# Pooled attention and expert routing on one core: values pooled inside their own pair, another order of loads and mixing steps, no unused matmuls

## The chip, the cores and the metric

The kernel runs on one NeuronCore of a Trainium2 chip. The metric is the device time of one execution in microseconds (us); runs are compared by their median. A core has five engines that work side by side, each with a queue that it takes in order: PE (TensorE, matrix products), DVE (VectorE), ACT (ScalarE), POOL (GpSimd, which here issues most DMA transfers) and SP (SyncE, which here issues the writes of one intermediate). PE's weight loads are listed by themselves as PEld.

## What is computed

Batch 8, 8 heads, 576 positions, head size 64. Keys and values are averaged over groups of 8 positions (576 become 72), attention runs against these 72, and its output, 4608 tokens of 512, goes through one of 8 experts of two layers, chosen for each token by a given index.

```python
k_p = k.reshape(B, H, Sp, pool, D).mean(axis=3)      # pool = 8, Sp = 72
v_p = v.reshape(B, H, Sp, pool, D).mean(axis=3)
scores = scale * np.matmul(q, k_p.transpose(0, 1, 3, 2))
attn = np.exp(scores - np.max(scores, axis=-1, keepdims=True))
attn = attn / (np.sum(attn, axis=-1, keepdims=True) + 1e-09)
x = np.matmul(attn, v_p)                             # then (B*S, H*D)
...
for e in range(E):
    mask = domain_id == e
    h = np.maximum(x[mask] @ w1[e], 0.0)
    out[mask] = h @ w2[e]
```

## The kernel before

**Staging.** The attention works on pairs of batches, four pairs (`NP`). For each pair the three inputs are loaded as one tile of 128 partitions each, 1152 KB in half precision (`load_pair`, L78), issued on GpSimd's queue; each of k, q and v has two buffers, so that the load for pair 2 waits until pair 0's tile has been read. All of PE's work is cut into small units, and a plan puts them in order:

- `kp_units` (L373): pools k by 16 matmuls against an identity matrix (L392) and turns the result (L400); two copies out of PSUM for each, on VectorE, or on ScalarE in pair 0 (L383, L385). Six units.
- `vp_units` (L406): nine units pool and turn v by four matmuls each (L421), with three copies on ScalarE (L424); two more units fold pairs of positions into one (L434), with a copy each on ScalarE (L436). The result `vp` has two buffers, the intermediate `vT` one.
- `qt_units` (L440): five units transpose q (L449); four copies on VectorE (L453), one on ScalarE (L451).
- `sc_unit` (L456): scores of one head for all 576 positions, two matmuls (L463), then the exponential on ScalarE (L466). 16 for each pair.
- `av_unit` (L469), here called a mixing step: 8 or 16 matmuls (L483) mix the pooled values by the scores for 128 tokens into the PSUM tile `wide`, of which there is one; VectorE divides by the sums (L487, L489) into `x_sb`. 9 for each pair. After each third one SyncE writes 384 KB to the DRAM buffer `x_lin` (L498).
- `turn_units` (L549): transposes gathered tokens (L557) through a PSUM tile that shares the one buffer of `wide`; VectorE copies it to `xT` (L558).
- `l1_units` (L567) and `l2_units` (L588): the two layers of an expert (L578, L594). The result of the second is scattered to the output by GpSimd (L603).

**Order.** Each unit is put into a list with a number as its time (16 to a pair: pair `pr` has `16*pr` to `16*pr + 16`), the list is sorted, and the units are emitted in that order (L621 to L684). Each engine then takes its instructions in the order of emission. Score units of pair `pr` stand at `16*pr + h`. Mixing steps follow from 8.6 on, 16/9 apart, so that the last five of a pair fall into the next pair's numbers. Pooling and transposing for pair `pr + 1` stand inside pair `pr`: keys, values, queries, in this order (L637 to L641). Pair 0's values are pooled inside pair 0 too (L652).

**Routing.** While the attention runs, VectorE builds from the expert index the row of `x_lin` that each slot of an expert holds: `perm_units` and `perm_mm` for each pair, then `perm_finish` (L355, nine small operations), `orig_finish` (L367, nine) and `count` (L239, with one matmul, L248). Rows are fetched by indirect DMAs (`gather`, L542), five blocks of 128 for each expert. The first three blocks of experts 0 and 1 hold rows of the first three pairs alone, so these six gathers and expert 0's first layer on 384 tokens (`e0_unit`, L677) start while the fourth pair is still mixed.

**GpSimd's queue** is in order as well. Its loads before: k0, q0, v0, k1, v1, q1, then k2, v2, q2, k3, v3, q3, two weight loads (expert 0), six gathers, two weight loads (expert 1), and then gathers, loads and scatters of the expert stage.

**Unused matmuls.** `dummy` (L501) multiplies the identity by a part of k into a PSUM tile that nobody reads. Twelve of them stand at 48.4 to 59.4, in the fourth pair.

Of the kernel before, what the change touches and what calls it, by code (L numbers as in the profile page):

```python
# [20 lines left out]
NP = 4  # L21
NC_ = 9
# [11 lines left out]
XE = 128 * NC_ * EPAIR  # L34
# [5 lines left out]
def kernel(  # L40
# [10 lines left out]
    nc = tc.nc  # L51
# [19 lines left out]
    def small():  # L71
        return ps.tile([128, 512], F32, tag="small", bufs=2, name="small")
# [5 lines left out]
    def load_pair(t_ap, pr, tag):  # L78
        t = wp.tile([128, 72, D], F16, tag=tag, bufs=2, name=tag)
        nc.gpsimd.dma_start(  # L80
            t[:].rearrange("p t d -> p (t d)"),
            t_ap[2 * pr:2 * pr + 2].rearrange("b h (g t) d -> (b h g) (t d)", g=8))
        return t

    with tc.manual_schedule():
# [7 lines left out]
        kt, vt, qt_ = {}, {}, {}  # L93
# [13 lines left out]
        nc.gpsimd.iota(row_i[:], pattern=[[128, NCH]], base=0, channel_multiplier=1)  # L107
        vt[0] = load_pair(v, 0, "v")
        kt[1] = load_pair(k, 1, "k")
        vt[1] = load_pair(v, 1, "v")  # L110
        qt_[1] = load_pair(q, 1, "q")

        iota_f = rt.tile([128, 128], F32, name="iota_f")
        nc.vector.tensor_copy(iota_f[:], iota_row[:])
# [4 lines left out]
        ident = const.tile([128, 128], F16, name="ident")  # L119
# [26 lines left out]
        for cc in range(NC_):  # L146
            if cc <= 4:
                nc.tensor.matmul(Rv[:, :, cc, :], selA[:, 128 * cc:128 * cc + 128], domT[:, :, 0, :],
                                 start=True, stop=(cc < 4), skip_group_check=True)
            if cc >= 4:  # L150
                c0 = 128 * (cc - 4)
                nc.tensor.matmul(Rv[:, :, cc, :], selB[:, c0:c0 + 128], domT[:, :, 1, :],
                                 start=(cc > 4), stop=True, skip_group_check=True)
# [302 lines left out]
        def sc_unit(pr, bh):  # L456
            s = st[pr]
            if bh % 8 == 0:
                s["at", bh // 8] = wk.tile([128, H, S], F16, tag="at", bufs=3, name="at")
            at = s["at", bh // 8]  # L460
            p = big()
            for par in range(2):
                nc.tensor.matmul(p[0:72, par, 0:288], s["kpT"][64 * par:64 * par + 64, bh, :],  # L463
                                 s["qT"][64 * par:64 * par + 64, :, 8 * bh:8 * bh + 8],
                                 start=True, stop=True)
            nc.scalar.activation(at[0:72, bh % 8, :].rearrange("p (a c) -> p a c", a=2),  # L466
                                 p[0:72, :, 0:288], AFT.Exp, scale=1.0 / 64.0)

        def av_unit(pr, cc):  # L469
            s = st[pr]  # L470
            if cc % 3 == 0:
                s["x"] = per.tile([128, 3, HD], F16, tag="x_sb", bufs=4, name="x_sb")
            x_sb = s["x"][:, cc % 3, :]
            pv = wide()
            lo, hi = 128 * cc, 128 * cc + 128
            parts = []
            if lo < S:
                parts.append((0, lo, min(hi, S), 0))
            if hi > S:
                parts.append((1, max(lo, S) - S, hi - S, max(lo, S) - lo))  # L480
            for bt, a, z, r0 in parts:
                for h in range(H):
                    nc.tensor.matmul(pv[r0:r0 + z - a, h, 0:65], s["at", bt][0:72, h, a:z],  # L483
                                     s["vp"][0:72, 8 * bt + h, :], start=True, stop=True,
                                     skip_group_check=True)
            rcp = wk.tile([128, 8], F32, tag="rcp", bufs=4, name="rcp")
            nc.vector.reciprocal(rcp[:], pv[:, :, 64])  # L487

            nc.vector.tensor_tensor(out=x_sb.rearrange("p (b h a) -> p b h a", b=4, h=H),  # L489
                                    in0=pv[:, :, 0:64].rearrange("p h (a b) -> p b h a", b=4),  # L490
                                    in1=rcp[:].unsqueeze(1).unsqueeze(3).to_broadcast([128, 4, 8, 16]),
                                    op=ALU.mult)
            if cc % 3 == 2:
                if pr < EPAIR:
                    rows, c = x_lin[0:XE, :].rearrange("(p c) d -> p c d", c=EC), NC_ * pr + cc - 2
                else:
                    rows, c = x_lin[XE:XROWS, :].rearrange("(p c) d -> p c d", c=LC), NC_ * (pr - EPAIR) + cc - 2
                i = nc.sync.dma_start(rows[:, c:c + 3, :], s["x"][:])  # L498
                tc.declare_no_dep(i.ins, group="xg", reason="the rows gathered so far are of other pairs")

        def dummy():  # L501
            p = small()
            nc.tensor.matmul(p[:], ident[:], kt[NP - 1][:].rearrange("p t d -> p (t d)")[:, 0:512],
                             start=True, stop=True)

        def merge(a, b, start=0.0):

            out_, n = [], len(a)
# [15 lines left out]
        def wload_units(e, which, parts):  # L524
            box = {}

            def unit(i):
                if i == 0:
                    tag = W_AT[e][which]
                    bufs = 4 if tag == "w" else 2  # L530
                    t = wp.tile([128, 4096] if tag == "w" else [128, 72, D], F16, tag=tag, bufs=bufs, name=tag)
                    box["t"] = t[:] if tag == "w" else t[:].rearrange("p t d -> p (t d)")[:, 0:4096]
                    k = (4, 8)[which]
                    box["s"] = (moe_w1, moe_w2)[which][e].rearrange("(p k) f -> p (k f)", k=k)
                    wt.setdefault(e, []).append(box["t"].rearrange("p (k f) -> p k f", k=k))
                c = slice(4096 // parts * i, 4096 // parts * (i + 1))
                nc.gpsimd.dma_start(box["t"][:, c], box["s"][:, c])
            return [lambda i=i: unit(i) for i in range(parts)]
# [3 lines left out]
        def gather(e, j, rows=XROWS):  # L542
            i = nc.gpsimd.indirect_dma_start(  # L543
                out=xg[e % 2][:, j, :], out_offset=None, in_=x_lin[0:rows, :],
                in_offset=bass.IndirectOffsetOnAxis(ap=xrow[:, NBL * e + j:NBL * e + j + 1], axis=0),
                bounds_check=rows - 1, oob_is_err=False)
            tc.add_to_no_dep_group("xg", i.ins)
# [62 lines left out]
        def run(units):  # L610
            for f in units:
                f()
# [9 lines left out]
        plan = []  # L622

        def put(units, k0, k1):
            for i, f in enumerate(units):
                plan.append((k0 + (k1 - k0) * (i + 0.5) / len(units), len(plan), f))
# [4 lines left out]
        for pr in range(NP):  # L631
            t0 = 16.0 * pr
            for h in range(16):
                plan.append((t0 + h, -1, lambda pr=pr, h=h: sc_unit(pr, h)))
            for j in range(NC_):
                plan.append((t0 + 8.6 + j * 16.0 / 9.0, len(plan), lambda pr=pr, j=j: av_unit(pr, j)))
            if pr + 1 < NP:  # L637
                k0, k1, k2, k3 = (7.0, 10.0, 13.6, 15.7) if pr == 0 else (2.5, 6.5, 11.6, 14.8)
                put([lambda pr=pr, i=i: run(kp_units_(pr + 1, i)) for i in range(6)], t0 + k0, t0 + k1)
                put([lambda pr=pr, i=i: run(vp_units_(pr + 1, i)) for i in range(11)], t0 + k1, t0 + k2)  # L640
                put([lambda pr=pr, i=i: run(qt_units_(pr + 1, i)) for i in range(5)], t0 + k2, t0 + k3)  # L641
        made = {}

        def part(kind, f):
# [4 lines left out]
            return g  # L649
        kp_units_, vp_units_, qt_units_ = part("k", kp_units), part("v", vp_units), part("q", qt_units)  # L650
        put([ovf_mm, slot_post], 0.2, 1.0)
        put([lambda i=i: run(vp_units_(0, i)) for i in range(11)], 2.6, 6.6)  # L652
        put([perm_prep], 17.3, 17.3)
        for i in range(NP):
            put(perm_units(i), 18.0 + 8 * i, 25.0 + 8 * i)
            put([lambda i=i: perm_mm(i)], 26.5 + 8 * i, 26.5 + 8 * i)
        put([perm_finish], 52.0, 52.0)
        put([orig_finish], 58.0, 58.0)
        put([count], 61.0, 61.0)
        for h in range(12):  # L660
            put([dummy], 48.4 + h, 48.4 + h)
        for pr in range(2, NP):
            for d, t_ap, tag, kx in ((kt, k, "k", 5.0), (vt, v, "v", 9.0), (qt_, q, "q", 13.0)):
                put([lambda d=d, t_ap=t_ap, pr=pr, tag=tag: load(d, t_ap, pr, tag)],
                    16 * pr - 32 + kx, 16 * pr - 32 + kx)
        put(wload_units(0, 0, 1), 30.0, 30.0)
        put(wload_units(0, 1, 1), 33.0, 33.0)
        put([lambda j=j: gather(0, j, XE) for j in range(3)], 57.0, 60.0)
        put([lambda j=j: gather(1, j, XE) for j in range(3)], 60.0, 63.0)
        put(wload_units(1, 0, 1) + wload_units(1, 1, 1), 63.1, 63.2)  # L670
        put([lambda i=i: run(turn_units_(0, i)) for i in range(2)], 62.0, 64.0)
        def turn_units_(e, i):
            return [turn_units(e, 0, 3)[i]]
# [37 lines left out]
        for e in range(2, E):  # L711
            h = hidden()
# [10 lines left out]
            t = turn_units(e + 1, 0, NBL) if e + 1 < E else []  # L723
# [6 lines left out]
    with tc.If(nblk > 0), \  # L730
# [8 lines left out]
        with tc.For_i(0, nblk, 1):  # L739
# [37 lines left out]
            with tc.For_i(0, E, 1) as e:  # L777
# [8 lines left out]
                for fi in range(8):  # L786
                    hp = ovp.tile([128, 128], F32, name="ov_hp")
                    for kk in range(4):
                        nc.tensor.matmul(hp[:], w1[:, FF * kk + fi:FF * kk + FF:8], xT[:, kk, :],
                                         start=(kk == 0), stop=(kk == 3))  # L790
# [49 lines left out]
```

## Time and profile before

| what | value |
|---|---|
| median of 14 runs | 288.31 us (286.41 to 291.33) |
| the profiled execution, timed | 290.94 us |
| its span, first to last instruction | 289.1 us |
| granted TensorE clock, mean over the span | 0.923 |
| PE busy | 242.2 us (84%) |
| DVE busy | 124.9 us (43%) |
| ACT busy | 93.1 us (32%) |
| POOL busy | 98.0 us (34%) |
| moved by DMA | 50.19 MB |

Times inside the execution are us from the first instruction. The attention takes TensorE from about 12 to about 115 us; from 107 on the first layer of expert 0 runs between its last mixing steps. Experts 0 and 1 follow in two parts each until 151.6 us, and from 159 us on the six others, one after the other. Busy time counts matmuls from start to modelled end and so overlaps; to cost a unit, the distance between starts is used. The granted clock is that of TensorE as a share of full speed; in this trace it is either 1 or 0.5 at any moment.

### The profile page before, as it was taken

How to read it: one execution, taken by the hardware profiler on the slowest of the kernel's cores; microseconds unless marked ns; L12 is line 12 of the kernel's file. 1: busy time of each engine (PE TensorE's matmuls, PEld its weight loads, DVE VectorE, ACT ScalarE, POOL GpSimd, SP SyncE). 2: the span in 40 equal slices, each digit the busy share in tenths (PEclk: the TensorE clock that was granted, in tenths of full speed). 3: DMA queues.
4: the chain of work that ended last, by engine and by line, in shares of the span. 5: the costliest groups of instructions: out<-in, count | busy, mean ns of one | idle time of the engine just before them, and what ended most of it. 6: DMA issues, size and time to landing. Idle time of an engine off the chain costs nothing.

```text
span 289.1 us, 5003 instructions
## 1 busy us (share of the span) xinstructions
PE 242.2 (84%) x2060; PEld 168.4 (58%) x2060; DVE 124.9 (43%) x284; ACT 93.1 (32%) x157; POOL 98.0 (34%) x116
## 2 busy tenths in 40 slices
PE   0878979979888759889893999979978979888992
PEld 0766755755654337466742774945945945845940
DVE  7341566886887744342321234223233233234320
ACT  1047564674676514122200111211210211211310
POOL 6001020000000450174147725725725725624033
PEclk9997995996999557999997799999999999999997
DMA  6999999999991369459714999889689589513012
GB/s 115 215 216 214 218 222 242 230 242 245 233 245 71 107 162 221 134 111 252 209 65 102 221 255 209 250 150 172 215 152 179 182 161 177 199 42 116 19 74 103
DMA packets 10985, 50.19 MB, mean 174 GB/s; under 512 B 2316, under 2 KB 2382, under 8 KB 7376
## 3 DMA queue, kind: packets, MB, share of 16 engines
q0 software_dynamic: 9152, 45.10, 69.3%
q1 hardware_dynamic: 1808, 4.76, 4.4%
q8 instruction: 16, 0.26, 0.3%
q14 instruction: 9, 0.07, 0.1%
HBM read 67.15 MB, written 15.20 MB: 285 GB/s over the span
## 4 chain that ended last, share of the span: by engine, by line
PE 55%; issue 15%; DVE 10%; DMA 7%; POOL 6%; ACT 4%; POOLq 1%
PE big L578 21%; PE small L594 14%; DMA v<-in_v_dram 6%; POOL out_dram L603 5%; PE wide L483 4%; PE small L421 3%; PE small L392 3%; PE turn L557 3%; PE big L463 3%; DVE x_sb L489 2%; DVE xT L558 2%; PE small L449 2%; ACT vT L424 1%; ACT qT L451 1%; DMA xg<-x_lin,xrow 1%
## 5 line engine op out<-in xcount | busy, mean ns | idle before, releaser
L543 POOL DMA_INDIRECT xg<-x_lin,xrow x40 | 40.5, 1012 | 80.4 <-DVE rcp L487 53.6
L603 POOL DMA_INDIRECT out_dram<-y,tok x40 | 39.9, 998 | 72.5 <-DVE y L599 33.8
L466 ACT ACTIVATE at<-big 72x576 f16<-72x576 f32 x64 | 40.5, 644 | 33.1 <-PE big L463 33.0
L584 DVE TENSOR_SCALAR hT<-big 128x640 f16<-128x640 f32 (+1 forms) x32 | 23.2, 724 | 57.5 <-PE big L578 49.8
L578 PE MATMUL big<-xT,w 128*128 128x320 f16 (+2 forms) x256 | 41.4, 309 | 7.6 <-DVE xT L558 4.0
L594 PEld LDWEIGHTS <-hT 128*128 128x128 f16 x272 | 26.2, 98 | 28.3
L578 PEld LDWEIGHTS <-w 128*128 128x128 f16 x256 | 33.7, 146 | 12.7 <-issue 8.1
L582 ACT ACTIVATE hT<-big 128x640 f16<-128x640 f32 (+1 forms) x32 | 19.9, 623 | 63.3 <-PE big L578 57.4
L601 ACT ACTIVATE y<-small 128x512 f32<-128x512 f32 x20 | 11.9, 597 | 65.0 <-PE small L594 45.8
L599 DVE COPY y<-small 128x512 f32<-128x512 f32 x20 | 13.8, 692 | 36.0 <-PE small L594 34.9
L489 DVE TENSOR_TENSOR x_sb<-wide,rcp 128x512 f16<-128x512 f32 x36 | 24.9, 692 | 1.2
L594 PE MATMUL small<-w,hT 128*128 128x512 f16 x112 | 25.3, 379 | 0.0
L463 PE MATMUL big<-qT,kpT 64*72 64x288 f16 x128 | 21.8, 345 | 1.5 <-DVE qT L453 1.5
L558 DVE COPY xT<-turn 128x1024 f16<-128x1024 f16 (+1 forms) x24 | 14.4, 598 | 19.7 <-PE turn L557 19.7
L483 PE MATMUL wide<-vp,at 72*128 72x65 f16 (+1 forms) x320 | 18.1, 209 | 4.9 <-DVE x_sb L489 3.4
L483 PEld LDWEIGHTS <-at 72*128 72x128 f16 (+1 forms) x320 | 14.5, 110 | 11.4 <-DVE x_sb L489 6.7
L578 PE MATMUL big<-xT,k 128*128 128x320 f16 x128 | 20.0, 316 | 1.0 <-DVE xT L558 1.0
L557 PE MATMUL turn<-ident,xg 128*128 128x128 f16 x160 | 14.3, 230 | 7.4 <-DMA xg<-x_lin,xrow 4.3
L578 PEld LDWEIGHTS <-k 128*128 128x128 f16 x128 | 17.7, 146 | 2.8 <-issue 1.5
L557 PEld LDWEIGHTS <-xg 128*128 128x128 f16 x160 | 11.4, 102 | 13.2 <-DMA xg<-x_lin,xrow 6.2
L594 PE MATMUL small<-v,hT 128*128 128x512 f16 x80 | 17.9, 379 | 0.0
L463 PEld LDWEIGHTS <-kpT 64*72 64x72 f16 x128 | 7.6, 112 | 10.7 <-issue 7.1
(142 smaller groups left out, 264.9 us busy)
## 6 DMA issues: line engine op xcount, KB each, us to landing
w<-in_moe_w_dram POOLq DMA_DIRECT2D x8, 1024.0 KB
k<-in_k_dram POOLq DMA_DIRECT2D x4, 1152.0 KB
q<-in_q_dram POOLq DMA_DIRECT2D x4, 1152.0 KB
v<-in_v_dram POOLq DMA_DIRECT2D x4, 1152.0 KB
x_lin<-x_sb SPq DMA_DIRECT2D x12, 384.0 KB, 9.3
k<-in_moe_w_dram POOLq DMA_DIRECT2D x3, 1024.0 KB
v<-in_moe_w_dram POOLq DMA_DIRECT2D x3, 1024.0 KB
q<-in_moe_w_dram POOLq DMA_DIRECT2D x2, 1024.0 KB
```

Of the source, the lines that this page charges most:

```text
L463: nc.tensor.matmul(p[0:72, par, 0:288], s["kpT"][64 * par:64 * par + 64, bh, :], s["qT"][64 * par:64 * par + 64, :, 8 * bh:8 * bh + 8], st ...
L466: nc.scalar.activation(at[0:72, bh % 8, :].rearrange("p (a c) -> p a c", a=2), p[0:72, :, 0:288], AFT.Exp, scale=1.0 / 64.0)
L483: nc.tensor.matmul(pv[r0:r0 + z - a, h, 0:65], s["at", bt][0:72, h, a:z], s["vp"][0:72, 8 * bt + h, :], start=True, stop=True, skip_group_ ...
L489: nc.vector.tensor_tensor(out=x_sb.rearrange("p (b h a) -> p b h a", b=4, h=H), in0=pv[:, :, 0:64].rearrange("p h (a b) -> p b h a", b=4), ...
L543: i = nc.gpsimd.indirect_dma_start(out=xg[e % 2][:, j, :], out_offset=None, in_=x_lin[0:rows, :], in_offset=bass.IndirectOffsetOnAxis(ap=x ...
L557: nc.tensor.transpose(p[:, j - a, kk, :], xg[e % 2][:, j, 128 * kk:128 * kk + 128], ident[:])
L558: nc.vector.tensor_copy(xts[e][:, :, 128 * a:128 * z].rearrange("p k (j c) -> p j k c", c=128), p[:, 0:z - a])
L578: nc.tensor.matmul(p[:, a, 0:m], w1[:, kk, fi:FF:8], xT[:, kk, s0 + m * a:s0 + m * a + m], start=(kk == 0), stop=(kk == 3))
L582: nc.scalar.activation(dst, p[:, 0:nh, 0:m], AFT.Relu)
L584: nc.vector.tensor_scalar(out=dst, in0=p[:, 0:nh, 0:m], scalar1=0.0, scalar2=None, op0=ALU.max)
L594: nc.tensor.matmul(p[:], hT[:, fi, 128 * j:128 * j + 128], w2[:, fi, :], start=(fi == 0), stop=(fi == 7))
L603: i = nc.gpsimd.indirect_dma_start(out=out, out_offset=bass.IndirectOffsetOnAxis(ap=orig[0][:, bl:bl + 1], axis=0), in_=y[:], in_offset=No ...
```

## The change

1. Values: pair `pr`'s `vp_units` move from inside pair `pr - 1` (from pair 1 on) to inside pair `pr`, at 2.6 to 6.6 of it, in the fourth pair at 3.6 to 8.4. Keys and queries of the next pair stay in the pair before it, at 7.5 to 11.0 and 11.6 to 15.2.
2. Loads: q of each pair is issued ahead of v; the loads of pairs 2 and 3 get earlier numbers.
3. Mixing: the third pair's last five steps stand at 16.1 to 19.3 instead of 15.7 to 22.8 of that pair, and the fourth pair's at 9.2 to 18.9 instead of 8.6 to 22.8.
4. The twelve unused matmuls go.
5. Three weight loads instead of two stand ahead of the six gathers, all at earlier numbers; the gathers stand two earlier, `orig_finish` and `count` one later.

What is computed and stored is the same.

```diff
         vt[0] = load_pair(v, 0, "v")
         kt[1] = load_pair(k, 1, "k")
+        qt_[1] = load_pair(q, 1, "q")
         vt[1] = load_pair(v, 1, "v")
-        qt_[1] = load_pair(q, 1, "q")
...
-        def dummy():
-            p = small()
-            nc.tensor.matmul(p[:], ident[:], kt[NP - 1][:].rearrange("p t d -> p (t d)")[:, 0:512],
-                             start=True, stop=True)
...
+            if pr + 1 < NP:
+                at = [8.6 + 1.78 * j for j in range(NC_)]
+                if pr == NP - 2:
+                    at[4:] = [16.1, 16.9, 17.7, 18.5, 19.3]
+            else:
+                at = [9.2, 10.4, 11.6, 12.8, 16.1, 16.8, 17.5, 18.2, 18.9]
             for j in range(NC_):
-                plan.append((t0 + 8.6 + j * 16.0 / 9.0, len(plan), lambda pr=pr, j=j: av_unit(pr, j)))
+                plan.append((t0 + at[j], len(plan), lambda pr=pr, j=j: av_unit(pr, j)))
+            k0, k1 = (2.6, 6.6) if pr < NP - 1 else (3.6, 8.4)
+            put([lambda pr=pr, i=i: run(vp_units_(pr, i)) for i in range(11)], t0 + k0, t0 + k1)
             if pr + 1 < NP:
-                k0, k1, k2, k3 = (7.0, 10.0, 13.6, 15.7) if pr == 0 else (2.5, 6.5, 11.6, 14.8)
-                put([lambda pr=pr, i=i: run(kp_units_(pr + 1, i)) for i in range(6)], t0 + k0, t0 + k1)
-                put([lambda pr=pr, i=i: run(vp_units_(pr + 1, i)) for i in range(11)], t0 + k1, t0 + k2)
-                put([lambda pr=pr, i=i: run(qt_units_(pr + 1, i)) for i in range(5)], t0 + k2, t0 + k3)
+                put([lambda pr=pr, i=i: run(kp_units_(pr + 1, i)) for i in range(6)], t0 + 7.5, t0 + 11.0)
+                put([lambda pr=pr, i=i: run(qt_units_(pr + 1, i)) for i in range(5)], t0 + 11.6, t0 + 15.2)
...
-        put([lambda i=i: run(vp_units_(0, i)) for i in range(11)], 2.6, 6.6)
...
-        put([orig_finish], 58.0, 58.0)
-        put([count], 61.0, 61.0)
-        for h in range(12):
-            put([dummy], 48.4 + h, 48.4 + h)
+        put([orig_finish], 59.0, 59.0)
+        put([count], 62.0, 62.0)
         for pr in range(2, NP):
-            for d, t_ap, tag, kx in ((kt, k, "k", 5.0), (vt, v, "v", 9.0), (qt_, q, "q", 13.0)):
+            for d, t_ap, tag, kx in ((kt, k, "k", -5.0), (qt_, q, "q", -0.6), (vt, v, "v", 7.0)):
                 put([lambda d=d, t_ap=t_ap, pr=pr, tag=tag: load(d, t_ap, pr, tag)],
-                    16 * pr - 32 + kx, 16 * pr - 32 + kx)
-        put(wload_units(0, 0, 1), 30.0, 30.0)
-        put(wload_units(0, 1, 1), 33.0, 33.0)
-        put([lambda j=j: gather(0, j, XE) for j in range(3)], 57.0, 60.0)
-        put([lambda j=j: gather(1, j, XE) for j in range(3)], 60.0, 63.0)
-        put(wload_units(1, 0, 1) + wload_units(1, 1, 1), 63.1, 63.2)
+                    max(0.1 + 0.1 * len(tag), 16 * pr - 32 + kx), max(0.1, 16 * pr - 32 + kx))
+        put(wload_units(0, 0, 1) + wload_units(0, 1, 1), 24.0, 25.0)
+        put(wload_units(1, 0, 1), 26.0, 26.0)
+        put([lambda j=j: gather(0, j, XE) for j in range(3)], 55.0, 58.0)
+        put([lambda j=j: gather(1, j, XE) for j in range(3)], 58.0, 61.0)
+        put(wload_units(1, 1, 1), 61.1, 61.1)
```

## The prediction

> **What bounds the kernel now.** I read the 40 slices first, then busy time per pair of the attention, then TensorE's order of time from 20 to 160 us, then the same in stretches of 3.41 us, the length at which the granted clock changes in this trace. The table of stretches lists core, length, busy time and instructions of PE, PEld, DVE, ACT and POOL, granted clock, DMA share, GB/s.
>
> ```profile
> PEclk9997995996999557999997799999999999999997
> DMA  6999999999991369459714999889689589513012
> ...
> 21.00:42.60 21.60, 18.78 (x269) 14.12 (x266) 8.68 (x24) 14.55 (x27) 2.69 (x6) 0.92 1.02 216
> 42.60:63.90 21.30, 19.16 (x243) 12.79 (x243) 16.88 (x43) 12.98 (x22) 1.00 (x2) 0.84 1.04 240
> 63.90:85.60 21.70, 19.18 (x252) 13.12 (x252) 17.48 (x42) 12.98 (x22) 0.00 (x0) 0.84 1.02 239
> 85.60:104.00 18.40, 14.02 (x126) 7.16 (x126) 13.69 (x52) 9.48 (x15) 5.32 (x6) 0.75 0.33 116
> ```
>
> Pairs 0, 1 and 2 are TensorE's: 19 of 21.5 us busy, at a clock that is partly half. DMA is full until 87 us, yet TensorE waits for a load only once (v of pair 0, at 22.16 us). The fourth pair is different: DMA is idle, TensorE has room, and a chain of mixing steps sets the pace. One mixing step `av_unit` (L483) fills the single buffer `wide`; the next can't start until L487 and L489 on VectorE have read it.
>
> ```profile
> 87.38 0.21 DVE L487 RECIPROCAL rcp<-wide 128x8 f32<-128x8 f32 x1
> 87.63 0.69 DVE L489 TENSOR_TENSOR x_sb<-wide,rcp 128x512 f16<-128x512 f32 x1
> 88.41 0.44 PE L483 MATMUL wide<-vp,at 72*128 72x65 f16 x8
> 89.87 0.43 PE L483 MATMUL wide<-vp,at 72*128 72x65 f16 x8
> 92.40 0.43 PE L483 MATMUL wide<-vp,at 72*128 72x65 f16 x8 [1.31 <-DVE x_sb L489]
> 102.48 1.01 PE L557 MATMUL turn<-ident,xg 128*128 128x128 f16 x8 [1.77 <-DVE meta L265]
> 107.07 1.50 PE L578 MATMUL big<-xT,w 128*128 128x384 f16 x4
> ```
>
> See the step: 88.41 to 89.87, 1.46 us, of which TensorE works 0.3. L503, the unused matmuls, stand in that gap and hold nothing up: at 88.41 the mixing step starts 0.09 us after its release. 92.40 is late because nine small VectorE operations (L357 to L365, 89.73 to 91.42) ran first. From 107.07 on TensorE is the bound again.
>
> **The change, part by part.** The sum runs from 20 us to the first layer of expert 0 (L578 at 107.07) and through it; span before 289.1 us.
>
> *Values out of pair 0: -3.5.* Before, pair 0 pools its own v and then pair 1's. That second set runs from 32.93 to 38.12 us, 5.19 us with three score steps (0.25 each from start to next start) and two mixing steps (0.27) among it, so 3.9 us alone, 0.8 of it idle.
>
> ```profile
> 32.93 0.40 PE L421 MATMUL small<-ident,v 128*128 128x128 f16 x4
> 36.97 0.74 PE L434 MATMUL small<-FI,vT 128*72 128x64 f16 x16 [0.39 <-ACT vT L424]
> 38.12 0.61 PE L449 MATMUL small<-ident,q 128*128 128x128 f16 x8 [0.40 <-ACT vp L436]
> ```
>
> The mixing steps, now closer together, take back some, as VectorE needs 0.95 us for each beside the four copies of q (2.2 us): bounds -2.6 (each step a full 1.46) and -4.5 (nothing but TensorE counts). I take -3.5, near the rows' own sum.
>
> *q ahead of v: 0.* The queue issues k, q, v for each pair. From the rates of the stretches (145, 213, 217, 214 GB/s in the first four of 10 us) five loads of 1.18 MB have landed at about 31 us and six at 36.5. q of pair 1 is now fifth and is first used at about 33.7; v of pair 1 is sixth and is first used at about 40.6. Cover: 2 and 4 us. In GpSimd's queue k and q of pair 2 go behind pair 1's v at once and wait there for the reads of pair 0; v of pair 3 waits for pair 1's last pooling (about 46 us), with three weight loads behind it, but by 46 us only eight of twelve loads have moved, so DMA has some 20 us of work in hand. If the cover for q were gone, each us late would be one on the path.
>
> *Pairs 1 and 2: -0.5.* The same instructions in another order; pooling of v now falls where the clock was half (43.5 to 50.3 us). There four key poolings took 1.25 us against 0.62, while twelve value poolings took 1.25 against 0.84 (24.30 and 54.75 us). Sixteen key poolings lose 1.7, thirty value poolings 1.0: at best -0.7 a pair; a second dip of 3.4 us at half clock costs 1.7. Bounds -1.4 and +1.7.
>
> *The fourth pair: +3.3.* Count from mixing step (third pair, 5 of 9) at 84.85 to L578 at 107.07: 22.2 us. After, in the order that the built kernel has: 2.06 (84.85 to 86.91) and three steps of 1.46, one of them with the permutation's matmul, bring the third pair's last step to +6.5 (before +7.55: the nine operations are now behind it). Then the fourth pair's eleven value units, with five score steps and no mixing, must end before its own mixing can begin; such a set took 5.2 us at 32.93, 6.0 at 52.08, 6.5 at 22.16: 6.0, where before the next mixing step came after 1.46. Then 1.46, 1.46, 2.5 (the nine L285 operations, 1.54 us, stand ahead of one L487), 1.46, and 0.7 for L244 to L248, which TensorE now meets ahead of the turn: 7.6, before 8.62. The turn to L578: 4.2 instead of 4.6, as the rest of `count` (1.5 us) holds the first xT copy while the turn runs. Together 24.3, or +2.1.
>
> The twelve L503 matmuls cost nothing where they stood, but they were TensorE's activity:
>
> ```profile
> 87.86:91.28 3.42, 3.23 (x38) 1.55 (x35) 2.82 (x12) 2.75 (x5) 0.00 (x0) 1.00 0.30 117
> 91.28:94.69 3.41, 2.29 (x25) 1.23 (x25) 2.23 (x7) 1.56 (x4) 0.00 (x0) 1.00 0.02 6
> 94.69:98.10 3.41, 3.35 (x25) 1.42 (x24) 2.75 (x12) 2.20 (x4) 0.94 (x1) 0.50 0.30 116
> 108.34:111.76 3.42, 3.42 (x24) 2.15 (x23) 0.90 (x2) 1.13 (x3) 0.00 (x0) 0.50 1.01 211
> 111.76:115.17 3.41, 3.41 (x38) 3.00 (x36) 1.80 (x4) 2.06 (x5) 0.00 (x0) 1.00 1.03 227
> ```
>
> A stretch with 2.29 of 3.41 us busy is followed by half clock (so are 40.1 to 43.5, 2.21, and 60.5 to 63.9, 2.38); full clock comes back after a stretch busy throughout. Without L503 a mixing step of 1.46 us holds 0.43 + 0.31 us of matmul, half busy: I expect half clock within one or two stretches of the pair's start instead of at 94.69. That costs 0.2 for each of four more mixing steps (0.62 against 0.43) and 0.4 for half of the value set: +1.2 with the bounds 0 and +2.5. Term: +3.3, bounds 0 (the value set shrinks to TensorE's own 3.9) and +5.
>
> The Trainium skill, "TensorE: Matmul & The Clock Gate", Part 1, speaks against this: it has the clock fall after an idle window of about 3.4 us, and warns of idle gaps of over about 3 us. Here the clock fell at 94.69 us with no gap over 1.31 us. By that page the removal of L503 is free and the term would be +2.1; I go by the row.
>
> *The first layer of expert 0: +1.9.* Before, five mixing steps stand one by one among its eight units, and it lasts 107.07 to 115.67. After, two of them (fourth pair, 6 and 7) are neighbours: the second waits 1.46 - 0.35 = 1.1 us, with the layer queued behind it. This gap puts off the first fully busy stretch by about 1.6 us on average, at half clock 0.8. Bounds 0 and +3.5.
>
> *At nothing.* The first gather follows the third pair's last write to DRAM: 93.8 to 97.16 before, now about 89.2 to 93.5, with 1 us added as the third weight load keeps DMA full to about 91 instead of 87. The gather's 5.3 us to the turn (97.16 to 102.48) then end at 99, and the turn comes at about 102: 3 us of cover. SyncE's queue holds only these writes. The fourth pair's writes land earlier, but the gather at 121.26 that waits for them feeds a turn at 128.24 that waited for no DMA. Expert 1's first weights move ahead of six gathers; its layer at 122.57 waited for xT. The gap at 151.6 to 159 follows from the scatters and gathers behind the second layer and moves with it.
>
> Sum: -3.5 - 0.5 + 3.3 + 1.9 = +1.2 us. The profiled execution took 290.94 us, 1.8 around its span, and lies 2.6 above the median of 288.31; I put the sum on the median: 289.5 us.
>
> **The rivals.**
>
> *Faster, 285.9 us.* The fourth pair's value set is dense, so the clock stays up through it and the first layer: the terms become -4.0, -0.5, +2.1 and 0 (1.1 of wait against 1.1 less of the 2.4 us that half clock costs from 107.07 to 111.76), together -2.4. For it: 6 us with fewer waits than any stretch after 91. Against it: four mixing steps at half density come right after.
>
> *An even exchange, about 288.3.* The set that leaves pair 0 (3.9) and the one that enters the fourth pair (4.5 over the step it replaces) cancel, and the clock's changes average out.
>
> *Late gathers, 291.2 us.* The third pair's last write shares DMA with the third weight load. Under load writes took 9.3 us; issued at 89.2 it would land at 98.5, the turn could not come before 103.7, about 1.7 later than above: +2.9 with the forecast's own 1.2. It decides once the first gather issues after 97. Against it: one load's 4.5 us is all that is added.
>
> *The change doing less than it says* is excluded by the order: the built kernel has each value set in its own pair, and no L503.
>
> **How the numbers follow.** Forecast 0.38, faster 0.32, even 0.20, late gathers 0.10. A measurement of this kernel can tell about 0.3% (0.9 us) from no change. Of the forecast's own chance 0.06 falls within 0.9 us, and of the even one 0.05 falls on either side: faster 0.37, same 0.16, slower 0.47. The range takes the terms' nearer bounds: 285.6 to 292.3; the forecast's own is 288.3 to 291.3.
>
> **What would show it.** Right: the fourth pair's first score step at about 82 us instead of 85.62 (wrong: later than 84); 6 us between the third pair's last and the fourth's first mixing step; half clock from about 85 to 88 us on; L578 at 106 to 108 us with a wait of about 1 us in front of a mixing step; the second layer of expert 0 at 116 to 118 instead of 115.67. A first L578 before 104.5, or full clock from 95 on, would make the prediction wrong toward faster; a turn that waits for xg would make it wrong toward slower.

## The result and the profile after

The changed kernel is slower: 292.48 us in the median of 10 runs (290.09 to 296.0) against 288.88 us before (47 runs), a ratio of 1.0119 with a 95% interval of 1.0086 to 1.0152: slower by 1.2%. Ratios compare only runs within 1.5% of the fastest of their kernel; the first profiled execution of before, at 290.94 us, is not one of them. The profiled execution of the changed kernel was timed at 292.12 us, its span is 290.1 us, the mean granted clock 0.926.

The slices of the page of the changed kernel, which answer to those of before:

```profile
PEclk9999999799958656999996699999999999999998
DMA  6999999999999366498215999889689589513022
```

DMA is full for one slice longer, and half clock has left the early slices but for one. Below are the stretches of the changed kernel, with the columns as before. They are cut at the first score step of pairs 0, 1, 2 and 3, at the first matmul of expert 0 and at its second layer; pair 3's first score step stands here 0.24 us before the third pair's fifth mixing step at 78.34:

```profile
20.04:37.67 17.63, 15.66 (x238) 11.12 (x238) 8.35 (x23) 12.91 (x22) 1.68 (x4) 1.00 1.03 216
37.67:59.01 21.34, 17.55 (x243) 12.47 (x243) 16.91 (x43) 13.10 (x22) 2.12 (x4) 0.92 1.03 241
59.01:78.10 19.09, 15.73 (x236) 11.16 (x235) 17.16 (x42) 13.17 (x22) 0.00 (x0) 1.00 1.03 242
78.10:104.88 26.78, 17.93 (x202) 12.18 (x203) 14.60 (x54) 12.18 (x21) 6.70 (x7) 0.66 0.72 184
104.88:116.18 11.30, 10.27 (x66) 6.38 (x65) 4.49 (x10) 3.39 (x7) 0.03 (x2) 0.60 0.76 175
```

And the same stretches of before, in the profile that the prediction was made from, with the third cut at the fifth mixing step:

```profile
20.11:42.61 22.50, 19.66 (x290) 14.88 (x290) 8.69 (x24) 15.09 (x27) 2.70 (x6) 0.92 1.02 216
42.61:63.91 21.30, 19.16 (x244) 12.79 (x243) 16.88 (x43) 12.98 (x22) 0.99 (x2) 0.84 1.04 240
63.91:84.85 20.94, 18.57 (x236) 12.52 (x236) 16.72 (x40) 12.84 (x22) 0.00 (x0) 0.84 1.03 241
84.85:107.07 22.22, 15.99 (x162) 8.91 (x163) 15.21 (x55) 10.27 (x17) 7.30 (x8) 0.72 0.40 121
107.07:115.67 8.60, 8.60 (x67) 6.17 (x66) 4.05 (x10) 3.43 (x7) 0.00 (x0) 0.73 0.99 210
```

The time moves between the stages that the prediction named: the first pair is 4.9 us shorter, the fourth pair, from the third pair's fifth mixing step to expert 0, 4.3 longer (26.5 against 22.2), the first layer of expert 0 2.7 longer. In this pair of profiles the second layer begins at 116.18 instead of 115.67 us, only 0.5 later. From there to expert 2 both kernels are alike (116.18 to 159.14 against 115.67 to 159.0). TensorE's order of time in the changed kernel shows both losses (start, length, line, operation, count, idle time before it and its cause; the code after the change is five lines shorter, so L573 is the first layer and L589 the second):

```profile
52.12 0.84 PE L449 MATMUL small<-ident,q 128*128 128x128 f16 x8 [2.20 <-DMA q<-in_q_dram]
...
84.93 0.62 PE L483 MATMUL wide<-vp,at 72*128 72x65 f16 x8
...
92.92 0.43 PE L483 MATMUL wide<-vp,at 72*128 72x65 f16 x8
...
104.88 1.50 PE L573 MATMUL big<-xT,w 128*128 128x384 f16 x4
106.39 0.62 PE L483 MATMUL wide<-vp,at 72*128 72x65 f16 x8
108.04 0.62 PE L483 MATMUL wide<-vp,at 72*128 72x65 f16 x8 [1.03 <-DVE x_sb L489]
108.47 1.47 PE L573 MATMUL big<-xT,w 128*128 128x384 f16 x4
```

Between 84.93 and 92.92, 8.0 us, only the value set and score steps run. At 106.39 and 108.04 two mixing steps are neighbours; the second waits 1.03 us, with the first layer queued behind it, and four of that layer's matmuls still take 1.47 us at 108.47 (at full clock they take 0.84 us, as at 108.53 in a row of a later run below). At 52.12 us there is a wait that the prediction did not have: q of pair 2 is not there yet. Two other profiles of the changed kernel, from the experiments below, don't show this wait.

### The profile page after: what moved, and what is told of

It is laid out like the page before. It is cut to its first block, busy times and chain, and to the rows that moved or that the text cites. A ratio compares the mean times of both kernels' runs of the same rounds, so it can differ in the third digit from the quotient of the medians.

```text
span 290.1 us, 4980 instructions
## 1 busy us (share of the span) xinstructions
PE 238.0 (82%) x2048; PEld 166.2 (57%) x2048; DVE 124.4 (43%) x284; ACT 93.3 (32%) x157; POOL 97.8 (34%) x116
## 4 chain that ended last, share of the span: by engine, by line
PE 28%; issue 26%; DMA 22%; POOL 11%; DVE 9%; ACT 1%; POOLq 1%
DMA q<-in_q_dram 16%; PE big L573 11%; POOL out_dram L598 6%; PE small L589 5%; DMA out_dram<-y,tok 5%; POOL xg L538 3%; PE wide L483 3%; DVE x_sb L489 3%; PE small L421 2%; PE big L463 2%; PE small L449 2%; DVE xT L553 1%; DVE qT L453 1%; DMA xg<-x_lin,xrow 1%; PE turn L552 1%
## 5 line engine op out<-in xcount | busy, mean ns | idle before, releaser
L573 PE MATMUL big<-xT,w 128*128 128x320 f16 (+2 forms) x256 | 42.1, 313 | 7.4 <-DVE hT L579 3.5
L589 PEld LDWEIGHTS <-hT 128*128 128x128 f16 x272 | 26.2, 98 | 28.3
L573 PEld LDWEIGHTS <-w 128*128 128x128 f16 x256 | 33.9, 145 | 13.1 <-issue 8.5
L483 PE MATMUL wide<-vp,at 72*128 72x65 f16 (+1 forms) x320 | 18.7, 210 | 9.1 <-DVE x_sb L489 8.2
L589 PE MATMUL small<-w,hT 128*128 128x512 f16 x112 | 25.3, 379 | 0.0
L463 PE MATMUL big<-qT,kpT 64*72 64x288 f16 x128 | 20.8, 332 | 3.0 <-DVE qT L453 2.8
L573 PE MATMUL big<-xT,k 128*128 128x320 f16 x128 | 20.8, 326 | 1.0 <-DVE xT L553 1.0
L573 PEld LDWEIGHTS <-k 128*128 128x128 f16 x128 | 17.9, 148 | 3.5 <-issue 1.5
L552 PEld LDWEIGHTS <-xg 128*128 128x128 f16 x160 | 11.6, 103 | 12.4 <-DMA xg<-x_lin,xrow 7.2
L589 PE MATMUL small<-v,hT 128*128 128x512 f16 x80 | 17.9, 379 | 0.0
L449 PE MATMUL small<-ident,q 128*128 128x128 f16 x144 | 11.7, 231 | 4.7 <-DMA q<-in_q_dram 3.1
```

The lines of the kernel that those rows point to most:

```text
L449: nc.tensor.transpose(p[:, j, :], qq[:, 128 * (j0 + j):128 * (j0 + j) + 128], ident[:])
L552: nc.tensor.transpose(p[:, j - a, kk, :], xg[e % 2][:, j, 128 * kk:128 * kk + 128], ident[:])
L573: nc.tensor.matmul(p[:, a, 0:m], w1[:, kk, fi:FF:8], xT[:, kk, s0 + m * a:s0 + m * a + m], start=(kk == 0), stop=(kk == 3))
L589: nc.tensor.matmul(p[:], hT[:, fi, 128 * j:128 * j + 128], w2[:, fi, :], start=(fi == 0), stop=(fi == 7))
```

## The experiments

The runs were made on four chips. The kernel before had a median of 280.18, 280.19, 279.63 and 283.15 us there, so across chips only ratios to before on the same chip are compared. Line numbers in the kernels made from the changed one are as in it, five higher where `dummy` was put back.

**A second profile of before.**

> The kernel before, unchanged, for a second profile. The first profile of it was timed 2 us above its median. If lost clock is the cause (the unused matmuls usually keep the clock up into the first expert layer), this profile shows full clock until later than 94.7 us or half clock for less than 17 us there, and its first expert layer starts before 106 us. If the serial value set of the fourth pair or a late load is the cause, the stretch from the fourth pair to the first expert layer looks as in the first profile, and the lower time comes from elsewhere.

279.38 us, 0.8 below that chip's median. Its stretches, cut at the same events:

```profile
20.25:42.52 22.27, 18.30 (x291) 13.78 (x290) 8.68 (x24) 15.04 (x27) 2.70 (x6) 1.00 1.02 215
42.52:63.95 21.43, 17.75 (x243) 12.76 (x243) 16.78 (x43) 13.11 (x22) 0.99 (x2) 0.92 1.03 238
63.95:82.54 18.59, 15.99 (x236) 11.44 (x236) 16.49 (x40) 12.85 (x22) 0.00 (x0) 1.00 1.03 244
82.54:103.92 21.38, 16.30 (x162) 9.02 (x163) 15.06 (x55) 10.29 (x17) 7.30 (x8) 0.71 0.51 147
103.92:112.54 8.62, 8.62 (x66) 6.19 (x65) 4.04 (x10) 3.44 (x7) 0.00 (x0) 0.72 0.99 201
```

Half clock was rarer in the first three stretches, and the second layer began at 112.54 instead of 115.67 us. The fourth pair and the first layer look as before, half clock included (91.7 to 108.7 us), in spite of the unused matmuls. Against this execution the changed kernel's 116.18 is 3.6 us late, as much as the difference of the medians (292.48 - 288.88 = 3.6). That the two agree so exactly is chance: in two other profiles of the changed kernel (a_same and a_same2 below) the second layer begins at 115.25 and 114.70, which is 2.7 and 2.2 us late. These profiles come from several chips.

**The unused matmuls**, taken from before (the diff shown), and given back to the changed kernel with the same lines:

```diff
-        for h in range(12):
-            put([dummy], 48.4 + h, 48.4 + h)
```

> The kernel before with the twelve unused matmuls taken out and nothing else. Lost clock as the main cause: slower by 1.5 to 3.5 us (0.5 to 1.2%). The serial value set or a late load as the cause: within 0.7 us of before (under 0.25%).

> The changed kernel with the twelve unused matmuls put back at their old numbers (48.4 to 59.4). Lost clock: 289.5 to 291, against 292.5 for the changed kernel. Serial value set or late load: 292 to 293.5, no better, as the value set still stands alone in the chain.

Without them before measures 1.0034 (0.9998 to 1.0071), about 0.9 us, not clear of nothing and between my two ranges. With them the changed kernel measures 1.0124 (1.0070 to 1.0179); by itself it measured 1.0135 and 1.0100 on other chips. Lost clock from these matmuls is not the main cause. The profile without them fits this: half clock begins at 86.8 us, earlier than the 91.7 and 94.6 of the two profiles of before, but the time from the third pair's fifth mixing step to expert 0 is 21.5 us against 21.4 in the second profile.

**The fourth pair's value set between the third pair's last mixing steps:**

```diff
-            k0, k1 = (2.6, 6.6) if pr < NP - 1 else (3.6, 8.4)
+            k0, k1 = (2.6, 6.6) if pr < NP - 1 else (0.1, 3.4)
```

> The changed kernel with the fourth pair's value set at 0.1 to 3.4 instead of 3.6 to 8.4, so between the third pair's last mixing steps, where TensorE waits for VectorE, instead of behind them. Serial value set (6 us in which no mixing step runs, against 1.5 before): faster than the changed kernel by 3 to 5 us, 287.5 to 289.5, so level with before or better. Lost clock: gains 1 to 2 us at most, by the denser stretch. A late load (q of pair 2, 2.2 us): unchanged within 1 us.

1.0064 (1.0034 to 1.0095): 0.5% under the changed kernel, some 1.6 us, where a serial value set as the cause was to give 3 to 5. The chain got shorter, but a new wait took much of it. Its first gather and its turn, from the timelines of GpSimd and TensorE:

```profile
96.68 1.08 POOL L538 DMA_INDIRECT xg<-x_lin,xrow  x1 [49.72 <-DVE nov_f L250]
```

```profile
94.33 0.62 PE L483 MATMUL wide<-vp,at 72*128 72x65 f16 x8 [1.37 <-DVE x_sb L489]
99.60 0.61 PE L552 MATMUL turn<-ident,xg 128*128 128x128 f16 x4 [3.12 <-DMA xg<-x_lin,xrow]
```

The mixing is done earlier, and the turn waits 3.12 us for gathered rows. The third pair's last write left at 86.31 us and the first gather could start only at 96.68: DMA was busy with the third weight load until about 95.

**The third weight load behind the gathers:**

```diff
-        put(wload_units(1, 0, 1), 26.0, 26.0)
...
-        put(wload_units(1, 1, 1), 61.1, 61.1)
+        put(wload_units(1, 0, 1) + wload_units(1, 1, 1), 61.1, 61.2)
```

> The changed kernel with the third weight load (expert 1's first) behind the six gathers, where before had it; nothing else. If the third load delays the third pair's last write and so the gathers (first gather at 96.7 us although that write was issued at 86.3): first gather near 93, and 0.5 to 1.5 us (0.2 to 0.5%) gained on the changed kernel's 1.0119. If the serial value set alone holds the turn back: nothing gained, as the turn then waits for the mixing steps.

1.0074 (1.0044 to 1.0103). The first gather starts at 91.20 us, 5 us earlier. The gain on the changed kernel is 0.3 to 0.6%, and the intervals overlap. The profile doesn't show where such a gain would come from: the turn begins 22.3 us after the third pair's fifth mixing step, as in the changed kernel (21.9 to 22.3 in three profiles), and it stands behind the mixing steps and `count`'s matmul, not behind a gather.

**The last mixing steps spread again over the first layer:**

```diff
-                at = [9.2, 10.4, 11.6, 12.8, 16.1, 16.8, 17.5, 18.2, 18.9]
+                at = [9.2, 10.4, 11.6, 12.8, 16.1, 17.5, 19.3, 21.0, 22.8]
```

> The changed kernel with the fourth pair's last four mixing steps back at 17.5, 19.3, 21.0 and 22.8, so that each has a unit of expert 0's first layer before it. If neighbouring mixing steps cost a wait and full clock there: the layer takes 8.6 to 9.2 us instead of 10 to 11.3, a gain of 1 to 2.5 us (ratio 1.003 to 1.008). If the layer's length is set by the clock alone: gain under 0.5 us.

0.9968 (0.9935 to 1.0002): this one list undoes the whole loss, more than I had expected. TensorE's order of time:

```profile
106.85 1.50 PE L573 MATMUL big<-xT,w 128*128 128x384 f16 x4
108.14 0.65 PE L483 MATMUL wide<-vp,at 72*128 72x65 f16 x8
108.60 2.14 PE L573 MATMUL big<-xT,w 128*128 128x384 f16 x8
110.57 0.42 PE L483 MATMUL wide<-vp,at 72*128 72x65 f16 x8
```

No wait stands in front of a mixing step, full clock is back at 110.0 us, 3.2 us after the layer's start (8.9 us after it in the changed kernel), and the layer takes 7.85 us (106.85 to 114.70).

**The same part alone in the kernel before, and the base beside it:**

```diff
-                plan.append((t0 + 8.6 + j * 16.0 / 9.0, len(plan), lambda pr=pr, j=j: av_unit(pr, j)))
+                plan.append((t0 + (8.6 + j * 16.0 / 9.0 if pr + 1 < NP or j < 4 else 16.1 + 0.7 * (j - 4)), len(plan), lambda pr=pr, j=j: av_unit(pr, j)))
```

> The kernel before with one part of the change alone: the fourth pair's last five mixing steps at 16.1, 16.8, 17.5, 18.2 and 18.9. If the neighbouring steps cost a wait and then full clock: the first layer of expert 0 takes 10 to 11.5 us instead of 8.6 and the ratio is 1.005 to 1.012. If they hurt only together with the moved value set: within 0.3% of before.

> The changed kernel, unchanged, beside the three others on one chip, as a base for them: ratio 1.008 to 1.015 to before. Under 1.006 the parts undone so far would have to be measured against this smaller loss, and the spread of the mixing steps would be worth less than the 1.5% that two chips gave.

On one chip: before 279.63 us, before with the five crowded steps 283.19 (1.0112, 1.0069 to 1.0154), the changed kernel 283.23 (1.0135, 1.0093 to 1.0177). The crowded steps alone cost about what the whole change costs. In the profile of before with crowded steps the same wait stands:

```profile
106.37 0.64 PE L483 MATMUL wide<-vp,at 72*128 72x65 f16 x8
108.04 0.62 PE L483 MATMUL wide<-vp,at 72*128 72x65 f16 x8 [1.03 <-DVE x_sb L489]
...
115.84 1.89 PE L594 MATMUL small<-w,hTe 128*128 128x512 f16 x8 [0.46 <-issue]
```

Its first layer lasts 105.07 to 115.84, 10.8 us, and so accounts for 2.2 of the 3.3 us by which the second layer begins later than in the second profile of before. The rest lies ahead of anything that the edit moves: the fourth pair took 1.9 us longer, with half clock from 84.2 us in this profile, and what precedes it 0.7 less. Over all profiles the layer takes 10.1 to 11.3 us with the crowded order (five kernels without filling) and 7.8 to 8.7 with one mixing step between two units of the layer, but for one below (a_spread_vp3, 10.4 us), where half clock lasted through nearly all of it.

**The wait filled** with two unused matmuls between the neighbours:

```diff
...
+        put([dummy, dummy], 64.85, 65.0)
```

(The cut line stands for `dummy`, put back as before.)

> The changed kernel with two unused matmuls (0.45 us each at half clock) in the wait between the two neighbouring mixing steps of the fourth pair. If the wait costs mostly by keeping the clock down: the layer shortens by 1 us or more, ratio 0.003 or more below the changed kernel's. If it costs by its own length alone: no gain, within 0.2% of the changed kernel.

1.0091 (1.0056 to 1.0127), 1.0 us under the changed kernel in the median, but the intervals overlap. Half clock ends at 108.4 us instead of 111.4 beside it, yet the layer takes 9.7 instead of 10.1 us:

```profile
108.21 0.48 PE L483 MATMUL wide<-vp,at 72*128 72x65 f16 x8 [0.17 <-DVE x_sb L489]
108.53 0.84 PE L578 MATMUL big<-xT,w 128*128 128x384 f16 x4
109.72 0.43 PE L483 MATMUL wide<-vp,at 72*128 72x65 f16 x8 [0.35 <-DVE x_sb L489]
```

At full clock one unit of the layer (0.84 us) no longer fills the time between two mixing steps, so the next ones wait as well. How the loss divides into waiting and half clock is not settled by this run.

The traces say more on it. Cut into stretches of 3.41 us at the changes of the clock, the 18 profiles have 62 returns to full clock between 15 and 150 us, and each follows a stretch in which TensorE was busy for at least 2.9 us (61 of them at least 3.1); a busy stretch alone did not always bring full clock. In the changed kernel the wait lies in the stretch from 106.99 to 110.40, with 2.38 us busy, so half clock goes on through the next one. In the spread kernel the stretch from 106.57 to 109.98 is busy throughout, and full clock follows it.

**How much is theirs: changed and spread kernel on one chip.**

> The changed kernel once more, on one chip with the three that follow: 1.010 to 1.015.

> The changed kernel with the last mixing steps spread, beside the changed kernel on one chip. If the neighbouring steps are the whole loss: 0.995 to 1.000, so 3 to 5 us under the changed kernel. If the stage that the profiles show (2.3 us shorter) is all they cost: 1.003 to 1.007.

285.78 us (1.0100, 1.0038 to 1.0163) and 282.90 (0.9984, 0.9945 to 1.0023): 2.9 us, 1.0%. By its ratio it lies in the first of my two ranges, by its microseconds just under it. The layers in the two profiles (10.20 us in one, 7.82 in the other) account for 2.4 of the 2.9 us. They also allow an estimate of the shares. Within the layer half clock lasts 6.5 us in one and 3.0 in the other. With spread steps the layer took 7.85 us with 3.2 us of half clock (a_spread), and 10.37 with 7.7 us and a wait of 0.52 (a_spread_vp3, below), so a microsecond of half clock costs about 0.44. Of the 2.4 us some 1.5 are then half clock, and the rest is the wait itself. This rests on four single profiles.

**Together.** The value set between, the weight load late, the mixing steps spread:

> The changed kernel with three parts undone or moved: the fourth pair's value set between the third pair's last mixing steps, the third weight load behind the gathers, the last mixing steps spread. If the serial set, the late gathers and the neighbouring steps are the three losses, they are regained together: 4 to 6 us, ratio 0.990 to 0.998. If they were not the causes, above 1.005.

> c_all3 once more: 0.983 to 0.992. Above 0.995 its first measurement was a chance of few runs.

> The spread one with the fourth pair's value set between the third pair's last mixing steps, the third weight load still ahead of the gathers. If the gathers then hold the turn back (as in a_vp3_between, 3.1 us of wait): gain on the spread one under 2 us, ratio 0.991 to 0.998. If they don't: as c_all3, 0.985 to 0.990.

0.9875 (0.9824 to 0.9926), and again 0.9885 (0.9835 to 0.9936), the medians 276.24 against 280.19 and 281.44 against 283.15 us: faster than both kernels. Without the late weight load the same gives 1.0008 (0.9965 to 1.0050), no better than the spread kernel on that chip (0.9984) and outside both of my ranges: with the steps spread, moving the value set gains nothing until the gathers are freed. Its first gather starts at 96.18 us and its turn at 99.10, after 1.39 us of waiting for gathered rows; the turn stands at 96.51 in the three together. In this profile the first layer also took 10.4 us, so the gathers need not be all of it. TensorE and GpSimd in the three together:

```profile
84.81 0.43 PE L483 MATMUL wide<-vp,at 72*128 72x65 f16 x8
...
88.68 0.62 PE L483 MATMUL wide<-vp,at 72*128 72x65 f16 x8
...
96.51 1.02 PE L552 MATMUL turn<-ident,xg 128*128 128x128 f16 x8
```

```profile
91.30 1.07 POOL L538 DMA_INDIRECT xg<-x_lin,xrow  x1 [45.51 <-DVE rcp L487]
```

Third pair's last to fourth pair's first mixing step: 3.9 us instead of 8.0. First gather at 91.30, and a turn that waits for no DMA.

Two attempts to gain more drew the fourth pair's score steps forward as well:

```diff
-                plan.append((t0 + h, -1, lambda pr=pr, h=h: sc_unit(pr, h)))
+                th = h if pr < NP - 1 else (0.45 * h if h < 8 else 4.0 + 0.7 * (h - 8))
+                plan.append((t0 + th, -1, lambda pr=pr, h=h: sc_unit(pr, h)))
```

The first (best1) mixes at 4.2, 5.6, 7.0, 8.4, 9.8, 11.2, 17.5, 19.3 and 21.0, with `perm_finish` at 51.4 and the other small operations behind the turn; the second (best2) mixes four times ahead of the turn (4.2, 5.6, 7.0, 8.4, then 16.1, 17.5, 19.3, 21.0, 22.8), with all small operations ahead of it.

> The same three, and the fourth pair's score steps drawn forward so that its first mixing step follows the third pair's last one, two more mixing steps ahead of the turn, orig_finish and count behind it. If the order of the fourth pair is what decides, its chain of mixing steps runs at 1.5 us a step without a gap, the first expert layer starts at 97 to 101 us where before had 104 to 107, and the ratio is 0.980 to 0.990. If the gathers stay late (first gather after 95), 0.995 or more.

> c_all3 with the fourth pair's score steps drawn forward, four mixing steps ahead of the turn, and the small operations of orig_finish and count ahead of the turn, where it waits for the gathers: first expert layer 0.5 to 1.5 us earlier than in c_all3, ratio 0.981 to 0.987. If the gathers bound it already in c_all3: no better than 0.9875.

0.9924 (0.9891 to 0.9956) and 0.9913 (0.9870 to 0.9956): both faster than before, neither better than the three together and neither in the range hoped for; expert 0 starts at 101.86 and 103.23 us, where the three together have 100.76 and 101.11. In both, the third pair's last mixing step comes 7.8 us after its fifth. In the two profiles of the three together it comes 6.9 and 7.6 us after, so this explains little; the cause is open.

## Why the prediction was right and wrong

**The direction and most of the mechanism held.** The kernel is slower because the value set that leaves pair 0 returns in the fourth pair, and because two mixing steps became neighbours in front of the first layer. Their wait was forecast at 1.1 us and measured at 1.03. The part up to the third pair's fifth mixing step was forecast 4.0 us shorter, and in three profiles of the changed kernel it is 4.2, 3.7 and 4.6 us shorter than in the second profile of before. Other events lie elsewhere than forecast: the fourth pair's first score step at 78.10 us (forecast about 82), half clock from 79.7 (85 to 88), 8.0 us between the third pair's last and the fourth's first mixing step (6), the first L573 at 104.88 (106 to 108). So it is partly luck that the second layer, forecast at 115.67 + 1.2 = 116.9, was measured at 116.18: an earlier start and a longer fourth pair cancel. The same holds for the profiled run's 290.94 + 1.2 = 292.1 us beside the measured 292.12.

**The step that failed is the fourth pair's term, "+3.3, bounds 0 [...] and +5".** From the third pair's fifth mixing step to expert 0 the changed kernel takes 26.5 us (26.4 and 26.6 in its two other profiles), where the second profile of before has 21.4: +5.1. The term was mis-sized in two places. The base of 22.2 us came from one execution, and it is 0.8 shorter in the second. And the value set took 8.0 us from one mixing step to the other (8.2 in the two other profiles), where I had put 6.0 and 0.4 for half clock. Half clock lay from 79.7 to 89.9 over most of it (80.8 to 91.0 and 80.2 to 90.4 in the others), and TensorE had no gap there in which to hide it. By an estimate from these times, half of the 5.0 us from 84.93 to 89.9, some 2.5 us, is half clock, not 0.4. The rest of that walk was close: third pair's last mixing step at +6.6 (forecast +6.5), first mixing step to the turn 7.35 (7.6, and 0.8 for half clock, which is therefore not seen), turn to L573 4.6 (4.2).

**A second error is the last step of the sum**, "I put the sum on the median: 289.5 us". The terms had been worked out against an execution that was 2.6 us above that median. The second profile of before reaches expert 0's second layer 3.1 us earlier than the first one, so part of what the first was long by lay in the stretches from which the terms were taken. Against the second profile the terms are -4.2 (forecast -4.0), +5.1 (+3.3) and, for the first layer, 8.6 to 11.3, +2.7 (+1.9): together +3.6, where the forecast had +1.2. With the two other profiles of the changed kernel the sum is +2.7 and +2.2.

**The first layer's term was about right in size**: +2.7 in this profile, +1.4 and +1.6 in the two others (10.06 and 10.20 us against 8.62), forecast +1.9. The wait is as forecast. Half clock lasted to 113.82 in this profile, for 8.9 us of the layer; in the others it lasted 6.2 and 6.5 us, in the two of before 4.7 and 4.9. The experiments make this the part that decides: its crowded steps alone cost 1.1%, spreading them gives 1.0 to 1.5% back, while the move of the values, loads and weight load nets to about nothing, as the near cancellation of -4.2 and +5.1 says.

**The price of the unused matmuls** (+1.2, bounds 0 and +2.5) agrees with the 0.9 us of taking them out, but that run doesn't tell it from zero. Nor do the profiles show an effect on the clock: it fell at 94.6, 91.7 and 84.2 us in three profiles with these matmuls (two of before, one of before with crowded steps), and at 86.8 in the one of before without. So no run here decides between my row and the idle window in the Trainium skill's "TensorE: Matmul & The Clock Gate", Part 1. That Part also tells of a kernel whose short idles between groups of matmuls made the clock go up and down, so it does not say that removing the matmuls is free, as I had read it. The traces show a fall without an idle window: in the second profile of before the clock fell at 91.65 us, after 3.41 us (88.24 to 91.65) of which TensorE was busy for 2.10, with no gap over 1.31. The other half of my row, that full clock comes back after a stretch busy throughout, has an exception in its own trace: 43.5 to 46.9 was busy throughout (3.40 of 3.40), and half clock went on to 50.4.

**Costs put at nothing.** q of pair 2 was not covered in this profile: I checked pair 1's loads only, and the faster first pair reached the eighth load as it landed (2.20 us at 52.12 us). It is inside the -4.2. The late gathers were real but small: first gather at 96.66 instead of 93.5 us, the turn's second block 0.75 us late in the profile. They became a bound only when the value set was moved (3.12 us).

**A row misread.** In "Pairs 1 and 2" I gave 1.25 us for twelve value poolings at 24.30 us; that row has 1.46. Thirty of them then lose 1.6 us at half clock instead of 1.0, and the best case is a gain of about 0.1 to 0.2 a pair instead of 0.7.

**The rivals.** "Faster" needed full clock in the fourth pair: it was half for most of it. "An even exchange" describes the moved value set, but not the crowded steps. "Late gathers" was the wrong mechanism for this kernel, though the right one for the next version.

## What to carry to other kernels

When each step of a chain must wait for another engine to empty a single buffer, and other work stands in the same queue, put one unit of that work between each two steps of the chain. Moving the steps together to finish the chain sooner makes the work behind them wait; here it cost about as much (1.1%) as the whole change. Work moved into a stretch that looks idle belongs in the gaps of its chain, not between the chain's halves, and what the chain feeds (here write, gather, turn) must not queue behind other transfers at that time. Take a second profile before pricing a change of one per cent: here two executions of one kernel differed by 3.1 us up to the second layer of expert 0, and two of the changed kernel by 1.5.

## What the runs showed that I had not expected

The same kernel took 288.9 us on the first chip or chips and 279.6 to 283.2 us on four others. The difference lies in the expert stage: from expert 2's second layer to the end 119.2 us (169.98 to 289.15) in the first profile of before and 110.9 us (166.67 to 277.59) in the second, both at nearly full clock. In the first, TensorE stops for 1.0 to 1.8 us in the first layers of four of these experts. Its matmul there waits for VectorE's copy of an earlier result (L584):

```profile
190.22 1.25 PE L578 MATMUL big<-xT,q 128*128 128x320 f16 x8 [1.74 <-DVE hT L584]
```

The copy itself waited for TensorE before it started (at 189.35 us, after the last matmuls ahead of it), so what came first is open. Four such waits, 6.4 us in all, stand in the first profile of before and in the profile of the changed kernel alike, and so left the ratio alone; the second profile of before has none.
